# Shorter assignment rounds, whole-pass rejection and evenly spaced gathers in a fused transform and mixture-of-experts kernel

## Chip, cores, metric

One core of a Trainium2 chip. The metric is the device time of one execution in microseconds (us). A time is a median over runs; "span" is the length of one profiled execution, about 1.9 us under its time. Engines carry the profile's names: PE is TensorE, PEld its weight loads, DVE VectorE, ACT ScalarE, POOL GpSimd.

## The reference, cut to what matters

```python
x = real(fft2(x))                       # (8, 2496, 256) -> 19968 tokens of 256
logits = x @ w_gate                     # 8 experts
cap = N // E                            # 2496 tokens per expert
for idx in argsort(-logits.flatten()):  # best score first
    tok, e = idx // E, idx % E
    if assigned[tok] < 0 and counts[e] < cap:
        assigned[tok] = e; counts[e] += 1
for e in range(E):
    out[assigned == e] = relu(x[assigned == e] @ w1[e]) @ w2[e]
```

The greedy assignment is the awkward part. The kernel replaces the sorted walk by rounds: every token proposes to its best expert that has not rejected it, every expert over its capacity rejects its lowest proposals, and so on until nobody is over.

## The kernel before

Tokens that are certain after a first pass are processed as 40 "early" tiles (five per expert, 384 tokens each). The assignment of the others runs beside these tiles, step by step, mostly on VectorE. When it has settled, the rows of the remaining tokens are known, and 16 "late" tiles follow; their token rows are fetched from HBM by indirect transfers that GpSimd issues. GpSimd also writes all output rows, again by indirect transfers. Of a tile:

```python
def gather(d):                       # a late tile: three indirect transfers
    ...
    for q in range((d["n"] + P - 1) // P):
        nc.gpsimd.indirect_dma_start(out=xg[0:nr, q, :], in_=t_dram,
                                     in_offset=IndirectOffsetOnAxis(ap=d["ids"](q, nr), axis=0))

def up(d, fcs):                      # hps: 128 x 384, two matmuls each, evicted by ACT or DVE (take)
    ...
def down(d, b0, group):              # ops: 8 matmuls, evicted into a ring of output tiles, then put
    ...
    ot = out_tile()                  # ring of 8; of 18 once the assignment has settled
    take(ot[0:nr, :], ops[0:nr, 0:D])
    put = nc.gpsimd.indirect_dma_start(out=out, out_offset=..., in_=ot[0:nr, :])
```

What drives the assignment is a generator. It yields the VectorE time that a step costs, or SYNC, and `pace` takes a few steps after each third of a tile. A SYNC (a "break") ends this step, so that the PE work of a third of a tile lies between a VectorE result and the matmul that reads it. When the generator ends at tile j, `settled(j)` notes that tile, and `feed` starts the gathers at the next one:

```python
def pace(j):
    credit[0] = min(credit[0] + 1.9, CREDIT)
    while credit[0] > 0.0 and not placed:
        c = next(todo, "end")
        if c == "end":
            settled(j)                        # placed = [j]; wider ring; deeper PSUM buffers
            return
        if c is SYNC:
            return
        credit[0] -= c
        ...
def feed(j):
    ...
    while m < len(late) and placed and j >= min(max(placed[0] + 1 + (3 * m) // 2, 0 if m < 8 else 32), 38 + m):
        gather(late[m])
        ...
```

In the profile's lines hps and ops are the two matmul groups of a tile, sps those that sort tokens into tiles, inv_ps the inverse permutation that finds the late rows, trun, s_part and lists_x the assignment's thresholds, search and lists, xg, xl and xs the fetched rows, tp their transposes; zball holds output tiles and weights; dd and wa hold output tiles once the assignment has settled.

A round is `choose` (reject and pick the best expert), `lowest` (the eight lowest proposals per partition and expert), `search` (a search for the threshold by comparing 1,024 elements per turn) and `settle`.

## Time and profile before

| | before |
|---|---|
| time, median of the first 3 runs | 548.45 us (547.43 to 548.97) |
| span of the profile that the prediction reads | 591.5 us |
| span of a second profile of the same kernel, taken later | 546.0 us |
| PE, DVE, ACT, POOL busy in the second | 467.9, 386.9, 345.6, 312.1 us |

The two profiles differ by 45 us. The first comes from an execution of 593.3 us, far slower than the timed ones, and the prediction, which had only that one, says so. The second profile (run b_again below) is of the timed kind; all comparisons with the changed kernel use it. Here are the span, GpSimd's slices (40 of 13.7 us, busy tenths) and the last line of its chain of work that ended last:

```profile
span 546.0 us, 11322 instructions
...
PE   0576759797799999999899959999999999999970
...
POOL 7888814443131754544344423467777777777775
...
DMA out_dram<-zball,rows_l 0%; POOL out_dram L1256 0%; POOLq L1347 0%
```

Three things are to be seen. PE is at 9 nearly throughout from the twelfth slice on, and idle in the last one. POOL stands at 7 from slice 28 to slice 39, never higher or lower. And the chain ends on a put of POOL (out_dram), not on PE, though it is cut off there. A constant 7 fits a queue that is always busy but has a fixed pause between its instructions (0.97 of every 1.28 us, as the timeline shows). The timeline of the same kernel (start, duration, engine, line, operation, in brackets the idle time before and what ended it) shows the first gather, the last PE work and the last puts:

```profile
358.83 1.01 POOL L1205 DMA_INDIRECT xg<-t_dram,ids_l  x1 [0.30 <-issue]
...
524.67 3.66 PE L1252 MATMUL ops<-w2t,hb 128*128 128x256 bf16 x32
...
528.37 0.38 ACT L990 ACTIVATE zball<-ops 96x256 f32<-96x256 f32 x1 [1.36 <-PE ops L1252]
...
539.40 0.97 POOL L1256 DMA_INDIRECT out_dram<-zball,rows_l  x1 [0.30 <-DMA out_dram<-zball,rows_l]
540.68 0.93 POOL L1256 DMA_INDIRECT out_dram<-zball,rows_l  x1 [0.30 <-DMA out_dram<-zball,rows_l]
```

PE has finished at 528.33, the last eviction (ACT, 528.37) at 528.75, and the put of that tile starts at 540.68, 11.9 us later. Each transfer takes POOL 0.97 us and a pause of 0.30. This is the backlog that the argument turns on.

### The profile page before, as it was taken

The page shows a single profiled execution, that of the slowest core. Times are in us where ns is not written, and L with a number is a line of the kernel's source. Part 1 is how long each engine was busy: PE and PEld are TensorE (multiplying, and loading weights), DVE is VectorE, ACT ScalarE, POOL GpSimd, SP SyncE. Part 2 cuts the span into 40 slices and gives each one's busy share as a digit, 9 for nine tenths or more (in the row PEclk, how much of TensorE's full clock was granted, in tenths as well). Part 3 has the DMA queues.
Part 4 walks back from the last instruction along what each step waited for, and adds up shares of the span by engine and source line. Part 5 has one row for each costly group of instructions (what it writes and reads, how often), then busy time and mean ns, then how long its engine had stood idle before and what let it go on. Part 6 is the DMA issues. An engine that isn't in the chain of part 4 may idle for free. (4 is left out here: it accounts for less than half of the span.)

```text
span 591.5 us, 11322 instructions
## 1 busy us (share of the span) xinstructions
PE 482.5 (82%) x4014; PEld 358.1 (61%) x4023; DVE 383.4 (65%) x1063; ACT 341.7 (58%) x786; POOL 310.8 (53%) x362
## 2 busy tenths in 40 slices
PE   0567778887899999998998798887787679687993
PEld 0444447775686667766765676655565457465772
DVE  7799864978889889798888762543332324343551
ACT  7789861454688778786777476443432334343551
POOL 7878540622226545343444245665666575656553
PEclk9998779999999999999999799999998989989997
DMA  8999835387698962222222223212222221112111
GB/s 270 314 282 305 252 62 83 109 292 207 203 280 162 240 148 90 91 94 89 89 90 95 69 89 98 71 54 76 66 65 70 67 75 55 61 53 66 65 55 48
DMA packets 35169, 74.63 MB, mean 126 GB/s; under 512 B 6115, under 2 KB 14349, under 8 KB 35104
## 3 DMA queue, kind: packets, MB, share of 16 engines
q0 software_dynamic: 23296, 42.10, 27.4%
q1 hardware_dynamic: 11808, 31.73, 15.9%
q8 instruction: 33, 0.54, 0.4%
q14 instruction: 32, 0.26, 0.1%
HBM read 51.26 MB, written 32.24 MB: 141 GB/s over the span
## 5 line engine op out<-in xcount | busy, mean ns | idle before, releaser
L990 ACT ACTIVATE hb<-hps 128x384 bf16<-128x384 f32 (+1 forms) x331 | 145.8, 492 | 77.1 <-PE hps L1229 61.0
L1252 PE MATMUL ops<-w2t,hb 128*128 128x256 bf16 (+1 forms) x1344 | 178.1, 277 | 0.1
L1252 PEld LDWEIGHTS <-hb 128*128 128x128 bf16 (+1 forms) x1344 | 134.3, 100 | 35.2 <-issue 1.9
L1256 POOL DMA_INDIRECT out_dram<-zball,rid x94 | 96.2, 1024 | 109.6 <-ACT zball L990 96.2
L1229 PE MATMUL hps<-xs,zball 128*128 128x384 bf16 x640 | 131.5, 330 | 19.3 <-issue 10.5
L1229 PEld LDWEIGHTS <-zball 128*128 128x128 bf16 x896 | 86.6, 99 | 87.0 <-issue 48.2
L994 DVE TENSOR_SCALAR hb<-hps 128x384 bf16<-128x384 f32 (+1 forms) x117 | 62.4, 546 | 69.4 <-PE hps L1229 45.2
L1229 PE MATMUL hps<-xt,zball 128*128 128x384 bf16 (+1 forms) x256 | 51.4, 329 | 16.8 <-issue 10.9
L990 ACT ACTIVATE zball<-ops 128x256 f32<-128x256 f32 x96 | 36.9, 385 | 46.8 <-PE ops L1252 26.0
L129 POOL DMA_INDIRECT xb<-in_x_dram,mir_i x40 | 53.0, 1326 | 14.0 <-issue 10.8
L285 PE MATMUL tp<-identf,xa 128*128 128x128 f32 x160 | 28.6, 345 | 21.2 <-issue 11.6
L990 ACT ACTIVATE xs<-sps 128x384 bf16<-128x384 f32 x73 | 32.4, 493 | 20.0 <-PE sps L1093 11.5
L285 PEld LDWEIGHTS tp<-identf,xa 128*128 128x128 f32 x160 | 24.2, 180 | 28.8 <-issue 13.9
L1093 PE MATMUL sps<-pt,xl 128*128 128x192 bf16 x320 | 34.4, 248 | 2.8 <-DVE pt L1071 1.8
L1021 POOL COPY stage<-stage 128x258 bf16<-128x258 bf16 x40 | 17.7, 446 | 35.8 <-DVE stage L1016 32.6
L1071 DVE TENSOR_SCALAR pt<-rampw,spot 128x193 bf16<-128x193 bf16 x160 | 32.2, 293 | 1.0 <-PE sps L1093 0.7
L1093 PEld LDWEIGHTS <-xl 128*128 128x128 bf16 x320 | 27.5, 99 | 8.1 <-issue 6.0
L1256 POOL DMA_INDIRECT out_dram<-zball,rows_l x23 | 22.3, 971 | 17.0 <-DVE zball L996 9.9
L996 DVE COPY zball<-ops 128x256 f32<-128x256 f32 (+1 forms) x21 | 8.9, 423 | 30.0 <-PE ops L1252 9.6
L1205 POOL DMA_INDIRECT xg<-t_dram,ids_l x24 | 23.1, 964 | 7.9 <-issue 7.9
L1019 ACT ACTIVATE stage<-stage 128x254 bf16<-128x254 bf16 x40 | 15.7, 414 | 15.8 <-DVE stage L1016 13.9
L287 ACT COPY zt<-tp 128x1024 f32<-128x1024 f32 (+1 forms) x24 | 20.2, 868 | 6.1 <-PE tp L285 6.1
(357 smaller groups left out, 783.5 us busy)
## 6 DMA issues: line engine op xcount, KB each, us to landing
t_dram<-stage SPq DMA_DIRECT2D x20, 512.0 KB
xl<-t_dram SPq DMA_DIRECT2D x20, 512.0 KB
xa<-in_x_dram SPq DMA_DIRECT2D x8, 1024.0 KB
w1raw<-in_moe_w_dram POOLq DMA_DIRECT2D x8, 512.0 KB
w2t<-in_moe_w_dram POOLq DMA_DIRECT2D x8, 512.0 KB
xa<-in_x_dram SPq DMA_DIRECT2D x8, 224.0 KB
out_dram<-zball,rid POOLq DMA_INDIRECT x94
xb<-in_x_dram,mir_i POOLq DMA_INDIRECT x40
```

What stands on the lines that cost most here:

```text
L129: nc.gpsimd.indirect_dma_start(out=bv[0:n, i, :], out_offset=None, in_=x_pairs, in_offset=bass.IndirectOffsetOnAxis(ap=mir_i[0:n, b * NK + ...
L285: nc.tensor.transpose(tp[:, blk, u, :], pv[:, 4 * c + u, blk * P:(blk + 1) * P], identf)
L287: nc.scalar.copy(zt[:, :, 0:nn, :], tp[:, :, 0:nn, :])
L990: nc.scalar.activation(dst, src, ACT.Relu if relu else ACT.Copy)
L994: nc.vector.tensor_scalar(dst, in0=src, scalar1=0.0, scalar2=None, op0=AL.max)
L1021: nc.gpsimd.tensor_copy(st[:, :, 1 + q, 0:P + 1], st[:, :, 3 * q, 0:P + 1])
L1071: nc.vector.tensor_scalar(marks[n][:, f, 0:EW + 1], in0=rampw[:, 0:EW + 1], scalar1=spot[:, c:c + 1], scalar2=None, op0=AL.is_equal)
L1093: nc.tensor.matmul(sps[:, j2 * EW:(j2 + 1) * EW], lhsT=xl[:, 2 * g + cc, j2 * P:(j2 + 1) * P], rhs=pt[:, 2 * g + cc, 0:EW], start=(cc == 0 ...
L1205: nc.gpsimd.indirect_dma_start(out=xg[0:nr, q, :], out_offset=None, in_=t_dram, in_offset=bass.IndirectOffsetOnAxis(ap=d["ids"](q, nr), ax ...
L1229: nc.tensor.matmul(hps[:, 0:n], lhsT=w1t[d["e"]][:, j2, fc * P:(fc + 1) * P], rhs=d["x"](j2), start=(j2 == 0), stop=(j2 == 1))
L1252: nc.tensor.matmul(ops[0:nr, 0:D], lhsT=d["hid"][:, fc, b0:b0 + nr], rhs=w2t[d["e"]][:, fc, :], start=(fc == 0), stop=(fc == F // P - 1))
L1256: put = nc.gpsimd.indirect_dma_start(out=out, out_offset=bass.IndirectOffsetOnAxis(ap=d["rows"](b0 // P)[0:nr], axis=0), in_=ot[0:nr, :], ...
```

## The change

Its intent is a shorter assignment beside the tiles:

- Rejection and choice are two whole passes over 8 x 160 elements instead of eight steps of 160 each. The choices are marked in bf16 and counted by ten PE matmuls rather than by VectorE's accumulator.
- From the second round on, lists of four per partition instead of eight, and two search turns instead of three; the first round loses its third search turn.
- 56 leftover tokens per partition instead of 64; the inverse permutation is computed in a layout with an inner run of eight, and gets one more break before its first matmul.
- Gathers are spread evenly from the settled tile to tile 52, in place of two in every three tiles.

```diff
 def choose(first):
-    for e in range(E):
-        nc.vector.tensor_scalar(wa[:, e, :], in0=lg[:, e, :], scalar1=tsel[:, e:e + 1], scalar2=0.0,
-                                op0=AL.add, op1=AL.min)
-        ...
-    nc.vector.scalar_tensor_tensor(wa, in0=wa, scalar=K_PEN, in1=lg, op0=AL.mult, op1=AL.add)
+    nc.vector.tensor_tensor(off, lg, tsel[:, :, None].to_broadcast([P, E, GC]), op=AL.is_lt)
+    nc.vector.scalar_tensor_tensor(wa, in0=off, scalar=-K_PEN, in1=lg, op0=AL.mult, op1=AL.add)
     ...
-    for e in range(E):
-        nc.vector.scalar_tensor_tensor(dd[:, e, :], in0=src[:, e, :], scalar=0.0, in1=mx, op0=AL.add,
-                                       op1=AL.is_lt, accum_out=cnt[:, e:e + 1])
-        ...
+    nc.vector.tensor_tensor(off, src, mx[:, None, :].to_broadcast([P, E, GC]), op=AL.is_lt)

 def count():
-    nc.tensor.matmul(cps[:, 0:1], lhsT=cnt_x, rhs=onesf, start=True, stop=True)
+    for c in range(0, GC, NG):
+        nc.tensor.matmul(cps[:, 0:P], lhsT=onesb, rhs=off[:, :, c:c + NG], start=(c == 0), stop=(c + NG == GC))

 def settle_rest():
-    yield from finish_round()            # search(1), then settle()
+    yield from settle()
     for _ in range(NROUND - 1):
-        yield from round_steps()         # lists of eight, search(3)
+        yield from round_steps(4, 2)

 # the inverse permutation
     yield SYNC
+    if c0 == 0:
+        yield SYNC
 # the eight keys of a step
-    yield 0.6
+    yield 0.75

 def feed(j):
-    ... placed[0] + 1 + (3 * m) // 2 ...
+    ... placed[0] + 1 + m * (51 - placed[0]) // 15 ...
```

(Cut: the penalty constant, raised from 1e16 to 1e20, other raised yields, the narrower lists in `lowest`, the inner-eight layout of the inverse, and the renaming of `dd` to `off`, a bf16 view of the same buffer, which the profile goes on calling dd.)

More of the change, by code (lines that the diff above doesn't have):

```diff
@@ L34 @@
 MAGIC = 12582912.0
-K_PEN = 1.0e16
+K_PEN = 1.0e20
 K_LOW = 1.0e30
@@ L53 @@
 CB = 20
-KC = 64
+KC = 56
 OT = 8
@@ L519 @@
     dd = asg.tile([P, E, GC], FT, name="dd")
+    off = dd.rearrange("p e c -> p (e c)").bitcast(BF)[:, 0:E * GC].rearrange("p (e c) -> p e c", c=GC)
     ohb = asg.tile([P, E, GC], BF, name="ohb")
@@ L522 @@
     tree = asg.tile([P, 4, GC], FT, name="tree")
-    cnt = asg.tile([P, E], FT, name="cnt")
     lists = asg.tile([P, E, 8], FT, name="lists")
     lists_x = asg.tile([P, 8, P], FT, name="lists_x")
-    cnt_x = asg.tile([P, P], FT, name="cnt_x")
+    cjunk = asg.tile([P, P], BF, name="cjunk")
     tsel = asg.tile([P, E], FT, name="tsel")
@@ L582, in choose @@
         else:
-            for e in range(E):
-                nc.vector.tensor_scalar(wa[:, e, :], in0=lg[:, e, :], scalar1=tsel[:, e:e + 1], scalar2=0.0,
-                                        op0=AL.add, op1=AL.min)
-                if e % 2 == 1:
-                    yield 0.5
-            nc.vector.scalar_tensor_tensor(wa, in0=wa, scalar=K_PEN, in1=lg, op0=AL.mult, op1=AL.add)
-            yield 1.4
+            nc.vector.tensor_tensor(off, lg, tsel[:, :, None].to_broadcast([P, E, GC]), op=AL.is_lt)
+            yield 1.5
+            nc.vector.scalar_tensor_tensor(wa, in0=off, scalar=-K_PEN, in1=lg, op0=AL.mult, op1=AL.add)
+            yield 1.5
             src = wa
@@ L595, in choose @@
         nc.vector.tensor_tensor(mx, mx, mv, op=AL.max)
-        yield 1.0
-        for e in range(E):
-            nc.vector.scalar_tensor_tensor(dd[:, e, :], in0=src[:, e, :], scalar=0.0, in1=mx, op0=AL.add,
-                                           op1=AL.is_lt, accum_out=cnt[:, e:e + 1])
-            if e % 3 == 2:
-                yield 1.05
-        nc.vector.tensor_copy(cnt_x.rearrange("p (e g) -> p e g", g=NG), cnt[:, :, None].to_broadcast([P, E, NG]))
-        yield 0.9
+        yield 1.2
+        nc.vector.tensor_tensor(off, src, mx[:, None, :].to_broadcast([P, E, GC]), op=AL.is_lt)
+        yield 1.5
         chosen["src"] = src
@@ L607, in count, with lowest @@
         cps = misc()
-        nc.tensor.matmul(cps[:, 0:1], lhsT=cnt_x, rhs=onesf, start=True, stop=True)
-        nc.vector.tensor_scalar(exc, in0=cps[:, 0:1], scalar1=-1.0, scalar2=float(P * GC - CAP), op0=AL.mult, op1=AL.add)
+        for c in range(0, GC, NG):
+            nc.tensor.matmul(cps[:, 0:P], lhsT=onesb, rhs=off[:, :, c:c + NG], start=(c == 0), stop=(c + NG == GC))
+        less = small("less")
+        nc.vector.scalar_tensor_tensor(cjunk, in0=cps[:, 0:P], scalar=-1.0, in1=bdiag, op0=AL.mult, op1=AL.mult,
+                                       accum_out=less)
+        nc.vector.tensor_scalar(exc, in0=less, scalar1=float(P * GC - CAP), scalar2=None, op0=AL.add)
     chosen, found = {}, {}
-    def lowest():
-        nc.vector.scalar_tensor_tensor(wa, in0=dd, scalar=-K_LOW, in1=chosen["src"], op0=AL.mult, op1=AL.subtract)
-        yield 1.4
+    def lowest(deep_):
+        nc.vector.scalar_tensor_tensor(wa, in0=off, scalar=-K_LOW, in1=chosen["src"], op0=AL.mult, op1=AL.subtract)
+        yield 1.5
+        step = 32 // deep_
         for e in range(E):
@@ L618, in lowest @@
             if e % 4 == 3:
-                es = slice(e - 3, e + 1)
-                nc.vector.tensor_copy(lists_x.rearrange("p j (e g) -> p j e g", g=NG)[:, :, es, :],
-                                      lists[:, es, :].rearrange("p e j -> p j e")[:, :, :, None].to_broadcast(
-                                          [P, 8, 4, NG]))
-                yield 1.8
+                yield 1.3
+            if (e + 1) % step == 0:
+                es = slice(e + 1 - step, e + 1)
+                nc.vector.tensor_copy(lists_x.rearrange("p j (e g) -> p j e g", g=NG)[:, 0:deep_, es, :],
+                                      lists[:, es, 0:deep_].rearrange("p e j -> p j e")[:, :, :, None].to_broadcast(
+                                          [P, deep_, step, NG]))
+                yield 0.5
         yield SYNC
         count()
-        lt = psr[0].tile([P, 8, P], FT, tag="lt", bufs=1, name="lt")
-        for j in range(8):
+        lt = psr[0].tile([P, deep_, P], FT, tag="lt", bufs=1, name="lt")
+        for j in range(deep_):
             nc.tensor.transpose(lt[:, j, :], lists_x[:, j, :], identf)
@@ L633, in lowest @@
         nc.vector.tensor_reduce(hi0, lt[:, 0, :], axis=AXX, op=AL.max)
-        nc.vector.tensor_reduce(lo0, lt[:, 7, :], axis=AXX, op=AL.max)
+        nc.vector.tensor_reduce(lo0, lt[:, deep_ - 1, :], axis=AXX, op=AL.max)
         wid = small("wid")
         nc.vector.tensor_tensor(wid, hi0, lo0, op=AL.subtract)
-        yield 0.7
-        found["low"], found["wid"], found["lo0"] = lo0, wid, lo0
+        yield 1.2
+        found["low"], found["wid"], found["lo0"], found["n"] = lo0, wid, lo0, deep_ * P
     def search(turns):
-        junk = wa.rearrange("p e c -> p (e c)")[:, 0:8 * P]
+        junk = wa.rearrange("p e c -> p (e c)")[:, 0:found["n"]]
         for _ in range(turns):
@@ L654, in search @@
             nc.vector.tensor_scalar(wid2, in0=part, scalar1=1.001, scalar2=None, op0=AL.mult)
-            yield 2.0
+            yield 0.9 + found["n"] / 850.0
             yield SYNC
@@ L665, in settle @@
         low, wid, lo0, ltf = found["low"], found["wid"], found["lo0"], found["ltf"]
-        junk = wa.rearrange("p e c -> p (e c)")[:, 0:8 * P]
+        junk = wa.rearrange("p e c -> p (e c)")[:, 0:found["n"]]
         top = small("top")
@@ L670, in settle @@
         nc.vector.tensor_scalar(junk, in0=ltf, scalar1=top, scalar2=0.0, op0=AL.is_gt, op1=AL.add, accum_out=n_top)
-        yield 1.5
+        yield 0.4 + found["n"] / 850.0
         nc.vector.scalar_tensor_tensor(junk, in0=junk, scalar=-1.0e34, in1=ltf, op0=AL.mult, op1=AL.add)
-        yield 1.2
+        yield 0.1 + found["n"] / 900.0
         best = small("best", 8)
         nc.vector.max(best, junk)
-        yield 1.1
+        yield 0.1 + found["n"] / 900.0
         left_ = small("left")
@@ L687, in settle @@
         nc.vector.tensor_tensor(trun, trun, tnew, op=AL.min)
-        yield 1.0
+        yield 1.6
         yield SYNC
@@ L691, in settle, with round_steps @@
         nc.tensor.transpose(bps[:, 0:P], trun.to_broadcast([P, P]), identf)
-        nc.vector.tensor_copy(tsel, bps[:, 0:P:NG])
+        nc.vector.tensor_scalar(tsel, in0=bps[:, 0:P:NG], scalar1=-1.0, scalar2=None, op0=AL.mult)
         yield 0.2
-    def finish_round():
-        yield from search(1)
-        yield from settle()
-    def round_steps():
+    def round_steps(deep_, turns):
         yield from choose(False)
-        yield from lowest()
-        yield from search(3)
+        yield from lowest(deep_)
+        yield from search(turns)
         yield from settle()
@@ L753, in inverse @@
             yield 0.65
-            o_hi = moe.tile([P, 8, EW + 2], BF, tag="pt", bufs=2, name="o_eq")[:, :, 0:w]
-            nc.vector.tensor_tensor(o_hi, rampw[:, None, 0:w].to_broadcast([P, 8, w]),
-                                    hi1[:, cs, None].to_broadcast([P, 8, w]), op=AL.is_equal)
-            nc.vector.tensor_tensor(o_hi, o_hi, pay[:, cs, None].to_broadcast([P, 8, w]), op=AL.mult)
-            yield 0.9
+            o_eq = moe.tile([P, 8, EW + 2], BF, tag="pt", bufs=2, name="o_eq")
+            if w <= P:
+                o_hi = o_eq.rearrange("p a b -> p (a b)")[:, 0:8 * w].rearrange("p (h c) -> p h c", c=8)
+                nc.vector.tensor_tensor(o_hi, ramp8[:, 0:w, :], hi1[:, None, cs].to_broadcast([P, w, 8]),
+                                        op=AL.is_equal)
+                nc.vector.tensor_tensor(o_hi, o_hi, pay[:, None, cs].to_broadcast([P, w, 8]), op=AL.mult)
+                o_hi = o_hi.rearrange("p h c -> p c h")
+            else:
+                o_hi = o_eq[:, :, 0:w]
+                nc.vector.tensor_tensor(o_hi, rampw[:, None, 0:w].to_broadcast([P, 8, w]),
+                                        hi1[:, cs, None].to_broadcast([P, 8, w]), op=AL.is_equal)
+                nc.vector.tensor_tensor(o_hi, o_hi, pay[:, cs, None].to_broadcast([P, 8, w]), op=AL.mult)
+            yield 0.8
             yield SYNC
+            if c0 == 0:
+                yield SYNC
             for c in range(8):
@@ L838, in first_strips @@
         nc.vector.scalar_tensor_tensor(sure, in0=mv, scalar=0.0, in1=sure, op0=AL.is_le, op1=AL.mult)
-        nc.vector.scalar_tensor_tensor(ohb, in0=dd, scalar=0.0, in1=sure[:, None, :].to_broadcast([P, E, GC]),
+        nc.vector.scalar_tensor_tensor(ohb, in0=off, scalar=0.0, in1=sure[:, None, :].to_broadcast([P, E, GC]),
                                        op0=AL.is_le, op1=AL.mult)
@@ L887, in first_chain @@
         yield from choose(True)
-        yield from lowest()
+        yield from lowest(8)
         yield from search(2)
@@ L898, in choose_rest @@
         count()
-        nc.vector.scalar_tensor_tensor(ohb, in0=dd, scalar=0.0, in1=rest[:, None, :].to_broadcast([P, E, GC]),
+        nc.vector.scalar_tensor_tensor(ohb, in0=off, scalar=0.0, in1=rest[:, None, :].to_broadcast([P, E, GC]),
                                        op0=AL.is_le, op1=AL.mult)
@@ L1318, in feed @@
             settled(j)
-        while m < len(late) and placed and j >= min(max(placed[0] + 1 + (3 * m) // 2, 0 if m < 8 else 32), 38 + m):
+        while m < len(late) and placed and j >= min(max(placed[0] + 1 + m * (51 - placed[0]) // 15, 0 if m < 8 else 32), 38 + m):
             gather(late[m])
@@ L1348 @@
         for _ in range(FALLBACK_ROUNDS):
-            run(round_steps())
+            run(round_steps(8, 3))
         run(choose(False))
@@ L1356 @@
             with tc.For_i(0, FALLBACK_LOOP):
-                run(round_steps())
+                run(round_steps(8, 3))
         run(choose_rest())
```

## The prediction

> **What bounds the kernel now.** I read the page first (busy shares and the forty slices), then the chain of work that ended last, then TensorE's waits by stretch, then the timeline of the one stretch where TensorE is weak, and last the groups of instructions of VectorE by shape.
>
> ```profile
> PE 482.5 (82%) x4014; PEld 358.1 (61%) x4023; DVE 383.4 (65%) x1063; ACT 341.7 (58%) x786; POOL 310.8 (53%) x362
> ...
> PE   0567778887899999998998798887787679687993
> ...
> DVE  7799864978889889798888762543332324343551
> ...
> PE 29%; issue 6%; POOL 2%; another core or an unknown queue 1%; ACT 1%; DVE 1%; POOLq 0%
> ```
>
> TensorE is the busiest engine and the chain that ended last runs along it: of what that chain names, 29% is TensorE and 1% VectorE. The row of slices (14.8 us each) has TensorE mostly at 9 from about 160 to 310 us, while VectorE, which works off the token assignment beside the experts, stays at 6 to 9 until about 355 us and then falls to 2 to 5. So the assignment, which is what this change rewrites, lies beside TensorE's matmuls. It costs time only where TensorE stands still for it.
>
> ```profile
> PE misc L658 <- DVE s_part L652: 2.1, 3, 1.1
> PE sps L1093 <- DVE pt L1071: 1.3, 2, 0.7
> PE lt L628 <- DVE lists_x L620: 0.8, 1, 0.8
> PE misc L691 <- DVE trun L687: 0.8, 1, 0.8
> ...
> PE inv_ps L761 <- DVE o_eq L757: 5.4, 1, 5.4
> ```
>
> These are TensorE's waits from 240 to 320 us (the first four; with two of 0.5 and 0.4 us for the slot scan they come to 5.9 us) and from 320 to 358 us (the last). They are all waits for VectorE's assignment. The largest single one is the first matmul of the inverse permutation. Its surroundings in the timeline:
>
> ```profile
> 322.03 1.04 PE L1252 MATMUL ops<-w2t,hb 128*128 128x256 bf16 x8
> ...
> 328.46 0.64 PE L761 MATMUL inv_ps<-o_eq,oh 128*128 128x48 bf16 x8 [5.40 <-DVE o_eq L757]
> ...
> 328.93 1.45 PE L1093 MATMUL sps<-pt,xl 128*128 128x192 bf16 x8
> ...
> 330.18 2.08 PE L1229 MATMUL hps<-xs,zball 128*128 128x384 bf16 x6
> ...
> 337.72 1.14 PE L1229 MATMUL hps<-xs,zball 128*128 128x384 bf16 x6
> ```
>
> After the 5.40 us hole, six hps matmuls take 2.08 us where six of them later take 1.14. The profile's loss in this place is therefore the hole plus about 1.6 us (0.94 there, and 0.6 in the sps group before it, which takes 0.82 us elsewhere).
>
> One warning on this profile: it spans 591.5 us, the timed runs take 548.45. The tiles between about 360 and 545 us are uneven in it (some start 5.3 us after the one before, some 10 us), the last five come every 5.3 to 5.5 us. If I add up 56 tiles at 5.45 us (305), 16 sorting calls of two groups at 0.82 us (26), four weight transposes of 3.4 (14), four row sums at 0.7 (3) and some 23 us of the assignment's own matmuls, and put them after the 173.8 us at which the first tile starts, I get 545. The timed run is close to that without any of those uneven gaps. So I take them for something that the profiled execution has and the timed one mostly lacks, and expect nothing from them.
>
> [...]in the table by stretches (each engine's busy time and count, then clock, DMA share and GB/s) the hole's stretch has a granted clock of 0.83 and its neighbours 1.00, and the matmuls above take almost twice as long.
>
> ```profile
> 300.00:320.00 20.00, 18.41 (x141) 13.34 (x142) 16.69 (x60) 14.70 (x37) 9.63 (x10) 1.00 0.26 85
> 320.00:340.00 20.00, 14.60 (x126) 11.32 (x125) 16.64 (x51) 10.21 (x25) 5.49 (x5) 0.83 0.18 61
> 340.00:360.00 20.00, 19.50 (x200) 15.38 (x200) 11.35 (x43) 14.78 (x38) 8.50 (x9) 1.00 0.25 83
> ```
>
> [...]
> [...]1,280 fp32 elements take 1,511 ns (the L588 group), while bf16 1,024 elements whose broadcasts keep an inner run of 8 take 685 ns (L751). But 384 bf16 elements with the broadcast on the inner dimension take 555 ns (L755)[...].
> [...]Here 160 elements take 302 to 320 ns, and an eighth of the 1,511 ns would be 189. That is the argument for whole passes.
> [...]
>
> **The change part by part.**
> VectorE. (1) Rejection and choice, five times over (the first without rejection): eight steps of 302 ns, eight counting steps of about 0.26 us start to start and a 0.27 us spread go; two passes of 1,280 elements at about 1.45 us (an estimate from the 1,511 and 1,483 ns rows) come. About 4.2 us become 2.9 in four of them, 2.4 become 1.45 in the first: 6 us saved. (2) The count now reads 128 columns from PSUM and reduces them: about 0.35 us more, five times, 1.7 lost. (3) Search: a turn takes 2.26 us in the timeline, of which 1,284 ns is the comparison of 1,024 elements; at 512 that is about 750 ns[...], so 1.73 a turn. Ten turns after the first strips become six: 22.6 less 10.4, 12 saved. (4) Settling on 512 elements in three rounds: three passes less 0.53 us each, 4.8 saved. (5) One spread copy of 434 ns less in three rounds: 1.3. (6) 56 keys for 64: one max and replace (0.7) and one chunk of eight of the inverse (1.8) less. (7) The inverse's two 384-element steps go to the inner-8 layout: 555 to about 357 ns, twice in seven chunks, 2.8 saved. Together 28 us of VectorE's 383. All of it lies beside TensorE.
> TensorE. Each count becomes ten matmuls of 128 columns[...] in place of one fp32 one (about 0.14)[...]. Twelve fp32 transposes less (eight take 1.07 us): 1.5 saved. Four search matmuls and eight inverse ones less: 0.9. Net 1 us more, on the path.
> Waits. The inverse gets one more break before its first matmul. A break lasts one third of a tile, 1.85 us between ops groups, and the yields before it are raised to what VectorE really needs (0.75 for 0.6 at each key step, 1.6 for 1.0 at the end of settling), so that VectorE is less behind when TensorE gets there. I expect 1 to 2 us to be left of 5.4, so 4 saved, and the 1.6 of slow clock with it. Of the other 5.9 us of waits in 240 to 320 us, the searching and settling ones should about halve, as there are 27 breaks for 31 and each has less VectorE work before it: 3 saved.
> Order. Stepping through the builder, the assignment ends at tile 20 and not at 24 (74 paced steps become some 60), so the deeper PSUM buffers and the wider ring of output tiles come four tiles sooner. TensorE idles little in those tiles, so half a microsecond. The gathers start at tile 21 and come every second tile to 52, instead of two in three from 25 to 47: GpSimd issues 4.5 instead of 5 indirect transfers a tile. At the 1.28 us spacing of such issues in the trace that is 5.8 us against 6.4, for a tile of 5.45; the ring of 18 output tiles takes up a lag of this kind. I put 1 us on it.
> First stage (100 to 175 us): about 0.6 us less VectorE work net, and TensorE's waits for it are short: 0.3.
> Sum: 4 + 1.6 + 3 + 0.5 + 1 + 0.3 less 1 is 9.4 us. [...]I take four fifths, 7.5: 548.45 becomes 541.
>
> Is the shortened assignment still complete? If it were not, the kernel would run its fallback[...]. I replayed both versions' rounds on the reference's scores: with four per partition, the second round rejects 112 of expert 7's surplus of 116, the third makes good, and after four rounds both versions end with no surplus. The fullest partition has 52 tokens left over, under 56. So no fallback.
>
> **The rivals.** (a) Nothing happens: VectorE was beside the path, and TensorE's added counts eat the small waits. For it speaks the chain (VectorE 1%); against it the 5.4 us hole, which is on TensorE in the middle of its busy stretch. It would give 545 to 549. (b) GpSimd is the true limit after tile 25: its indirect transfers stand back to back at 1.28 us while gathers run, and spreading them lifts a limit that the timed run has too. For it speak the uneven tiles of the profile; against it that adding up the work already gives the timed length. It would give 528 to 537. (c) The hole moves: with the assignment ending four tiles sooner, the same wait comes under a heavier load of sorting, or the ten count matmuls, which now wait on a whole pass, become a new hole of 1 to 2 us each. It would give 545 to 552; the raised yields speak against it.
>
> **Range and chances.** My middle is 541. (a) and half of (c) lie within 2%; 537.5 is the border to faster, and only (b), or all waits going at full value, gets there. I take 534 to 547.5 as the range for 8 in 10, faster by over 2% at 0.2, within 2% at 0.77, slower at 0.03.
>
> **What would show it.** Right: TensorE's wait at the inverse's first matmul under 2 us and the clock in that stretch at 1.00; the assignment's last VectorE step some 25 us sooner than 354.6; VectorE about 28 us less busy in all[...]. Wrong: a tail of tiles evenly faster after 360 us would mean rival (b); new waits of TensorE on the lines of the count would mean (c); a gain far over 9 us means that I undersized what the waits cost in the timed run; none at all means that the hole was made by the profile.

## The result, and the profile after

| | before | after |
|---|---|---|
| time, median | 548.55 us (547.43 to 548.97, 4 runs) | 535.99 us (535.51 to 536.25, 4 runs) |
| ratio of fast runs, 95% interval | | 0.9773 (0.9756 to 0.979) |
| span of the profile | 546.0 us (second profile) | 534.3 us |
| granted PE clock | 0.962 | 0.969 |
| DVE busy | 386.9 us | 372.7 us |

A ratio is the mean time of one kernel's fast runs over that of the other's fast runs of the same rounds, so it is not quite the ratio of the medians. The changed kernel is 2.3% faster: in the predicted range (534 to 547.5), 5 us under its middle, and just over the 2% line to which the prediction had given 0.2.

The same rows of the page, now of the changed kernel, with its chain:

```profile
span 534.3 us, 11232 instructions
...
PE   0567659899789899999899999999999999999983
...
POOL 7888815253122555555524336777677777777774
...
PE 70%; DVE 13%; ACT 9%; issue 4%; DMA 3%; POOL 1%; POOLq 0%; DVEq 0%; ACTq 0%
```

POOL's stretch of sevens begins two slices earlier (26 instead of 28, in slices of 13.4 us instead of 13.7), and the chain that ended last now runs along PE. The timeline answers to the lines shown of before:

```profile
328.16 1.01 POOL L1210 DMA_INDIRECT xg<-t_dram,ids_l  x1 [0.31 <-issue]
...
526.85 0.97 POOL L1261 DMA_INDIRECT out_dram<-zball,rows_l  x1 [0.30 <-issue]
528.13 0.93 POOL L1261 DMA_INDIRECT out_dram<-zball,rows_l  x1 [0.30 <-issue]
```

The first gather goes out at 328.16 instead of 358.83. The last put starts at 528.13, 1.5 us after its eviction instead of 11.9. PE itself ends at 526.19, only 2.1 us before the 528.33 of before, so most of the gain in these two spans cannot be PE's. PE's waits from 180 to 345 us (what waited, on what; total, count, longest, us) are these:

```profile
PE misc L601 <- DVE dd L594: 2.7, 1, 2.7
PE misc L690 <- DVE trun L686: 2.1, 1, 2.1
PE sps L1098 <- DVE pt L1076: 0.7, 2, 0.5
```

The 5.4 us wait before the inverse is gone. Two waits have taken its place in part: the ten count matmuls of the choice for the leftover tokens (the "second pass" of the expectations) wait 2.7 us for a whole VectorE pass, and the first settling waits 2.1 us. After the first the clock is lower, too: 0.91 from 260 to 280 us, with 1.00 in the 20 us before and after:

```profile
262.87 1.14 PE L1234 MATMUL hps<-xs,zball 128*128 128x384 bf16 x6
...
267.62 0.72 PE L601 MATMUL misc<-dd,onesb 128*128 128x128 bf16 x10 [2.74 <-DVE dd L594]
...
269.04 2.13 PE L1234 MATMUL hps<-xs,zball 128*128 128x384 bf16 x6
```

Six hps matmuls take 1.14 us before this hole and 2.13 us after it. In the second half, where b_again has no PE wait at all, two late gathers now hold PE:

```profile
PE tp L1222 <- DMA xs<-t_dram,ids_l: 2.3, 2, 1.4
```

Where the 11.7 us of the spans come from can be read along POOL's queue, because in the kernel before its transfers stand without a break from the first gather to the last put: 143 of them, (540.68 - 358.83) / 142 = 1.281 us apart.

| step | us |
|---|---|
| first gather, 358.83 to 328.16 | -30.7 |
| 155 transfers from there instead of 143 (12 more puts now fall after the first gather), 12 x 1.281 | +15.4 |
| pauses in the queue: 528.13 - 328.16 = 199.97, full it would be 154 x 1.281 = 197.3 | +2.7 |
| last put to end of span, 5.3 to 6.2 | +0.8 |
| sum | -11.7 |

The first gather is 30.7 us sooner because the assignment ends at tile 20 and not at tile 24 (tile 21 starts 24.3 us before tile 25, at 324.1 and 348.4) and because the tiles themselves come 6.4 us sooner (tile 25 at 348.4 instead of 354.85), as the hole before the inverse (5.4 us) and the slow clock after it (0.83 from 320 to 340 us in b_again, 1.00 here) are gone. This is arithmetic on two traces, and no two traces start alike: the first tile (its first hps matmul) starts at 171.5 us in b_again and at 172.1 here, and in the six kernels that share the same code up to that tile (this one and five below) it starts anywhere from 170.3 to 173.4. Differences of 1 to 3 us between two single traces are therefore read from the first tile, where that matters. Whether POOL's queue sets the end, and what each part of the change is worth, needed experiments.

### The profile page after: what moved, and what is told of

The parts are those of the page before. It is cut to its first block, busy times and chain, and to the rows that moved or that the text cites. A ratio compares the mean times of both kernels' runs of the same rounds, so it can differ in the third digit from the quotient of the medians.

```text
span 534.3 us, 11232 instructions
## 1 busy us (share of the span) xinstructions
PE 471.8 (88%) x4039; PEld 357.7 (67%) x4039; DVE 372.7 (70%) x952; ACT 337.9 (63%) x762; POOL 313.9 (59%) x362
## 4 chain that ended last, share of the span: by engine, by line
PE 70%; DVE 13%; ACT 9%; issue 4%; DMA 3%; POOL 1%; POOLq 0%; DVEq 0%; ACTq 0%
PE hps L1234 24%; PE ops L1257 24%; PE sps L1098 5%; PE fftps L1038 5%; PE wps L1058 2%; PE tp L285 2%; ACT zt L287 2%; DMA xa<-in_x_dram 2%; PE yps L295 1%; ACT tf L254 1%; POOL out_dram L1261 1%; DVE xa L343 1%; PE inv_ps L766 1%; DVE stage L1022 1%; PE tp L1222 1%
## 5 line engine op out<-in xcount | busy, mean ns | idle before, releaser
L1257 PE MATMUL ops<-w2t,hb 128*128 128x256 bf16 (+1 forms) x1344 | 175.3, 274 | 0.0
L1261 POOL DMA_INDIRECT out_dram<-zball,rid x85 | 89.3, 1051 | 82.7 <-ACT zball L995 63.8
L1234 PE MATMUL hps<-xs,zball 128*128 128x384 bf16 x640 | 127.3, 327 | 0.0
L999 DVE TENSOR_SCALAR hb<-hps 128x384 bf16<-128x384 f32 (+1 forms) x122 | 66.3, 549 | 47.2 <-PE hps L1234 39.2
L129 POOL DMA_INDIRECT xb<-in_x_dram,mir_i x40 | 54.3, 1357 | 11.9 <-issue 10.5
L995 ACT ACTIVATE zball<-ops 128x256 f32<-128x256 f32 (+1 forms) x79 | 30.4, 384 | 31.6 <-PE ops L1257 29.0
L1234 PE MATMUL hps<-xt,zball 128*128 128x384 bf16 (+1 forms) x256 | 48.4, 322 | 0.0
L995 ACT ACTIVATE xs<-sps 128x384 bf16<-128x384 f32 x68 | 30.4, 493 | 16.0 <-PE sps L1098 15.7
L1044 ACT COPY ev<-fftps 128x512 f32<-128x512 f32 x20 | 11.7, 584 | 22.9 <-PE fftps L1038 15.5
L1001 DVE COPY zball<-ops 128x256 f32<-128x256 f32 (+1 forms) x29 | 12.3, 424 | 19.4 <-PE ops L1257 19.4
```

The costliest lines, as they stand in the source:

```text
L129: nc.gpsimd.indirect_dma_start(out=bv[0:n, i, :], out_offset=None, in_=x_pairs, in_offset=bass.IndirectOffsetOnAxis(ap=mir_i[0:n, b * NK + ...
L995: nc.scalar.activation(dst, src, ACT.Relu if relu else ACT.Copy)
L999: nc.vector.tensor_scalar(dst, in0=src, scalar1=0.0, scalar2=None, op0=AL.max)
L1234: nc.tensor.matmul(hps[:, 0:n], lhsT=w1t[d["e"]][:, j2, fc * P:(fc + 1) * P], rhs=d["x"](j2), start=(j2 == 0), stop=(j2 == 1))
L1257: nc.tensor.matmul(ops[0:nr, 0:D], lhsT=d["hid"][:, fc, b0:b0 + nr], rhs=w2t[d["e"]][:, fc, :], start=(fc == 0), stop=(fc == F // P - 1))
L1261: put = nc.gpsimd.indirect_dma_start(out=out, out_offset=bass.IndirectOffsetOnAxis(ap=d["rows"](b0 // P)[0:nr], axis=0), in_=ot[0:nr, :], ...
```

## The experiments

Theory A: from the first gather on, GpSimd's queue of indirect transfers sets the end. A change in the assignment counts through the moment of the first gather. Theory B: TensorE sets the end, and the change counts by the holes that it takes out of TensorE. All runs gave correct results. In the expectations quoted below, the letters stand for what each text itself says.

**b_again: the kernel before, unchanged.** To see whether the first profile stands for the timed runs.

> The kernel before, unchanged, to have its profile a second time. If the uneven tiles of the first profile belong to how this kernel is profiled, the profile spans about 590 us again; if they were a chance event of one execution, it spans about 547 us and shows the timed run as it is. The timed runs are 548 us either way.

Measured: 548.41 us (18 runs), ratio 0.9997, span 546.0 us. The tiles from 360 us on start 5.2 to 5.9 us apart except for one step of 6.6, where the first profile has steps of 5.2 to 10.5. The uneven tiles do not belong to the timed kernel.

**b_even: the kernel before with the even spacing alone.**

```diff
-    ... placed[0] + 1 + (3 * m) // 2 ...
+    ... placed[0] + 1 + m * (51 - placed[0]) // 15 ...
```

> The kernel before with the evenly spaced gathers alone (tiles 25 to 52 in place of 25 to 47). Theory A, the gain comes from TensorE's waits for the assignment: within 1 us of 548. Theory B, GpSimd's queue of indirect transfers runs late after tile 25 and the gathers' spacing decides how late: 541 to 545 us.

Measured: 551.46 us, ratio 1.0069 (1.0052 to 1.0086), 0.7% slower: clear of the noise, though under the 2% that counts as slower. Neither theory expected it. The puts are prompt at the end (the last one 1.5 us after its eviction), but PE now waits, from 480 us on:

```profile
PE tp L1217 <- DMA xs<-t_dram,ids_l: 7.8, 5, 3.7
```

The last gathers are issued late into a queue that is full all the same, and PE stands for them and ends at 540.3 us instead of 528.3. The queue runs from 360.3 to 542.18 us, 143 transfers at 1.281: full in both orders. Spreading the gathers does not relieve the queue. It only decides whether puts or gathers are late. What makes the time longer is not shown by these traces: of the 2.3 us of span, 1.4 are a later first gather, up to which the two kernels are the same, and 0.8 lie after the last put.

**b_break: the kernel before with the additional break and the key share of 0.75.**

```diff
     yield SYNC
+    if c0 == 0:
+        yield SYNC
...
-    yield 0.6
+    yield 0.75
```

> The kernel before with the one more break before the inverse's first matmul and the key steps' yields at 0.75, nothing else. Theory A: the 5.4 us hole shrinks to 1 to 2 us and the clock stays up, 542 to 544 us. Theory B: under 2 us gained, 546.5 to 548.5 us.

Measured: 543.49 us, ratio 0.9921 (0.9904 to 0.9937). The wait falls from 5.4 us to this:

```profile
PE inv_ps L763 <- DVE o_eq L757: 1.9, 1, 1.9
```

The assignment still ends at tile 24, but the first gather goes out at 354.6 instead of 358.8, and with the same 143 transfers the last put starts at 536.21 instead of 540.68. The last put is again 11.8 us behind its eviction. So removing the hole brings 4.9 us in the median and 4.5 in the span, and both theories can claim it: PE ends 4.3 us sooner (524.01), and the queue as much. (The first tile happens to start 1.8 us later here, at 173.3; counted from there, both gain 6 us.)

**a_oldg: the changed kernel with the old gather spacing.** The b_even diff, reversed.

> The changed kernel with the old spacing of the gathers (tiles 21 to 43). Theory A: 535 to 537 us as the changed kernel. Theory B: 539 to 543 us, as GpSimd has 5 transfers a tile and falls behind by a microsecond a tile. A third possibility, that the last gather of the changed kernel is late and the old spacing avoids it: 532 to 534 us.

Measured: 533.59 us (530.79 to 535.42), ratio 0.9723 (0.9681 to 0.9765), in the range of the third possibility. The interval touches that of the changed kernel (0.9756 to 0.979), so the gain of half a per cent is likely but not settled by itself; b_even points the same way. PE has no wait from 480 us on, and the tiles keep their 5.2 to 5.6 us to the end. The queue is full: 155 transfers from 329.53 to 526.53, 1.279 us apart.

**a_rounds8, a_dup, a_nobreak and a_fix fell on another chip (number 5 in the record; the other experiments ran on 15, 8 and 6).** On it the kernel before takes 599.2 us (592.2 to 606.1, 39 runs), and its times spread by over 2%, so times of this group are not compared with the others. Three of the kernels were run again. What these runs do show is told first.

a_rounds8 (the changed kernel, old spacing, old rounds):

```diff
+    yield from search(1)
     yield from settle()
     for _ in range(NROUND - 1):
-        yield from round_steps(4, 2)
+        yield from round_steps(8, 3)
```

> The changed kernel with the old gather spacing, and with the old rounds put back (lists of eight, one search step): everything else of the change stays. The assignment then ends at tile 23 instead of 20 and the gathers start at tile 24 instead of 21. Theory A (GpSimd's backlog sets the end: what the rounds of four bring is an earlier start of the gathers): the last transfers come late again, the stretch from the last tile's start to the end grows from 17.9 us to about 22 or 23, and the time is 538 to 541 us against 533.6 of the same kernel with rounds of four. Theory B (the rounds only lie beside TensorE, their length costs nothing): 532 to 535 us.

a_dup (the changed kernel, old spacing, each late tile's first 128 rows fetched twice):

```diff
 def gather(d):
+    nc.gpsimd.indirect_dma_start(out=xg[0:P, 0, :], in_=t_dram,
+                                 in_offset=IndirectOffsetOnAxis(ap=d["ids"](0, P), axis=0))
     for q in range((d["n"] + P - 1) // P):
```

> The changed kernel with the old gather spacing, in which each of the 16 gathers' first 128 rows are fetched twice into the same place: 16 more indirect transfers on GpSimd's queue, the result unchanged. Theory A (GpSimd's queue of indirect transfers is full from tile 21 to the end): each adds its 1.285 us to the end, 16 x 1.285 = 20.6 us, so 551 to 555 us, with the last put far behind its eviction. Theory B (TensorE alone sets the end and the puts only trail by their latency): less than 3 us more, below 537 us.

a_nobreak (the changed kernel, even spacing, without the break):

```diff
     yield SYNC
-    if c0 == 0:
-        yield SYNC
...
-    yield 0.75
+    yield 0.6
```

> The changed kernel without the additional break ahead of the inverse's first matmul and with the old key share of 0.6; the rounds of four, the whole passes and the even spacing stay. Theory A (the break took away the hole, which also lowered the granted clock): a wait of 3 to 6 us before the inverse's matmul is back at about the 14th to 22nd tile, and the time is 538 to 542 us against 536 for the changed kernel. Theory B (the hole vanished because the rounds of four leave VectorE less loaded, the break is not needed): no such wait, 535 to 537 us.

a_fix (the changed kernel, old spacing, one break more):

```diff
 def choose_rest():
     yield from choose(False)
     yield SYNC
+    yield SYNC
     count()
```

> The changed kernel with the old gather spacing and with one more break: choose_rest's count matmuls are issued one tile later than the whole pass on VectorE that they read. Theory A (the 2.7 us hole at the second pass is on the path, as TensorE is full before it): the wait for dd is gone or below 0.5 us, and the time falls from 533.6 to 529 to 532 us. Theory B (GpSimd's queue is the true limit of the end, tiles before it have slack): the wait is gone, but the gathers start no earlier, and the time stays at 532.5 to 535 us.

Measured: a_rounds8 595.9 us (ratio 0.9987, 0.9955 to 1.002), a_dup 621.6 (one run), a_nobreak 602.35 (1.0043, 1.0011 to 1.0075), a_fix 591.92 (0.9868, 0.9819 to 0.9917). None of the times expected for the faster chip could be met here. The traces of this group have the look of the first profile, whose execution of 593.3 us lies in this chip's range, with tiles 5 to 13 us apart once the gathers run. In that first profile one such place reads:

```profile
446.09 0.55 DVE L994 TENSOR_SCALAR hb<-hps 128x384 bf16<-128x384 f32 x1
...
447.19 0.49 ACT L990 ACTIVATE hb<-hps 128x384 bf16<-128x384 f32 x1 [3.70 <-PE hps L1229]
447.54 0.98 POOL L1256 DMA_INDIRECT out_dram<-dd,rid  x1 [0.30 <-issue]
447.89 0.49 PE L1229 MATMUL hps<-xs,zball 128*128 128x384 bf16 x2
450.08 0.38 ACT L990 ACTIVATE zball<-ops 128x256 f32<-128x256 f32 x1 [2.40 <-remote]
```

From 447.7 to 450.1 VectorE and ScalarE stand still together (VectorE from 446.6), though the matmuls whose results they then evict had ended by 448.4; PE waits in turn. There are at least seventeen such common stops of 1.2 to 2.6 us in the first profile between 400 and 590 us, and in b_again none before PE's end. It is not that transfers are slower: in both traces the last DMA packet of an indirect transfer ends a median 1.1 to 1.2 us after POOL is done with it. The trace of the slow kind does hold only half as many records of landed transfers (244 on one queue's semaphore, against 528 in b_again). No run here shows why the engines stop, and the cause stays open. It is not needed for the change: the timed comparison was made where before takes 548 us.

The waits before 320 us, ahead of the gathers, can still be read. In a_nobreak:

```profile
PE misc L601 <- DVE dd L594: 2.7, 1, 2.7
...
PE inv_ps L764 <- DVE o_eq L754: 1.9, 1, 1.9
```

Without the break the wait before the inverse is 1.9 us, where 3 to 6 were expected: most of the old 5.4 us went with the rest of the change (lighter rounds, whole passes, the inner-eight layout; which of them is not separated), and the break takes the remaining 1.9. In a_fix the dd wait is gone. In a_rounds8 it is 1.2 us, but the search waits are back with 3.1 us in five.

**a_dup_again.** The decisive run for theory A, now where before takes 548.84 us.

> The kernel of the run a_dup once more, as that run fell on a chip on which the kernel before takes 599 us and not 548. On a chip on which before takes about 548: theory A (GpSimd's queue of indirect transfers is full from tile 21 to the end, so each of the 16 added ones moves the end by its 1.285 us): 551 to 556 us, no hps wait longer than before up to the gathers, and a put lag that grows to the end. Theory B (TensorE alone sets the end): below 537 us. If it falls on a slow chip again: 618 to 625 us.

Measured: 554.16 us (553.13 to 556.36), ratio 1.011, against 533.59 for the same kernel without the 16 transfers. That is 20.6 us, and 16 x 1.285 is 20.6. The agreement to a tenth is luck, as the runs of the two kernels spread by 3.2 and 4.6 us. The traces say it more closely: from the first gather to the last put it is 218.0 us here and 197.0 in a_oldg, 21.0 us for 16 more transfers. Each added transfer moved the end by its full place in the queue. Theory B's "below 537" is out. 171 transfers stand 1.282 us apart from 326.27 to 544.25. The backlog of puts grows until, at 460 us, all 18 output tiles of the ring wait for their put, 33 us behind. An ops tile can then not be evicted, and PE stops:

```profile
PE ops L1260 <- ACT wa L995: 4.6, 2, 3.3
PE ops L1260 <- ACT zball L995: 3.4, 1, 3.4
```

**a_rounds8_again.** What the rounds of four bring, everything else of the change being present.

> The kernel of the run a_rounds8 once more, as that one fell on a chip on which before takes 599 us. Compared with the 533.6 us of the same kernel with rounds of four (ratio to before 0.972). Theory A (GpSimd's queue of indirect transfers is full from the first gather to the end, as the 16 added transfers moved the end by 20.6 us; what the rounds of four bring is that the first gather goes out three tiles earlier): three tiles of 5.9 us later is some 17 us of queue time, of which the slack that the queue had at the end of the kernel with rounds of four is taken first; 538 to 543 us, ratio 0.980 to 0.990, and the stretch from the last tile's start to the end 22 us or more against 17.9. Theory B (the rounds only cost their waits): 532 to 535 us, ratio 0.969 to 0.975, last stretch unchanged.

Measured: 541.68 us (541.42 to 541.97), ratio 0.9875 (0.9853 to 0.9897), 8.1 us over a_oldg and in theory A's range. Its timeline and the last line of its chain:

```profile
348.07 1.01 POOL L1211 DMA_INDIRECT xg<-t_dram,ids_l  x1 [0.31 <-issue]
...
534.20 0.93 POOL L1262 DMA_INDIRECT out_dram<-zball,rows_l  x1 [0.30 <-DMA out_dram<-zball,rows_l]
```

```profile
DMA out_dram<-zball,rows_l 0%; POOL out_dram L1262 0%; POOLq L1353 0%
```

The last tile starts at 515.6 us, in a_oldg at 515.5, and PE ends at 523.38 against 523.27. That looks as if the rounds of four saved TensorE nothing, but the first tile starts at 170.6 us here and at 173.4 in a_oldg, with the same code up to it. Counted from the first tile, they save TensorE 2.9 us and bring the first gather forward by 21.4. As the two traces stand, the first gather comes 18.5 us sooner (348.07 to 329.53), at the price of nine more transfers behind it (11.5 us), and the last put moves by 7.7 us. The last put is 10.4 us behind its eviction here, 2.8 in a_oldg. Theory B could claim the 2.9 us; the times differ by 8.1.

**a_nobreak_again.**

> The kernel of the run a_nobreak once more, on a chip as the changed kernel had it, if one comes. On the slow chip its wait ahead of the inverse was 1.9 us and not the 5.4 of before, so the expectation of the first time, 538 to 542 us, is too high in its own terms. Theory A (the break brings only what that wait is, as most of the old hole went with the lighter rounds): 536 to 538 us against the 536.0 of the changed kernel, with a wait of about 1.9 us at the inverse. Theory B (GpSimd's queue sets the end, and without the break the assignment ends one tile sooner, so the gathers start sooner): 533 to 536 us in spite of the wait.

Measured: 539.63 us (539.17 to 539.79), ratio 0.9837 (0.9815 to 0.9859): 3.6 us over the changed kernel, above both theories' ranges. PE's waits from 180 to 345 us:

```profile
PE misc L601 <- DVE dd L594: 2.7, 1, 2.7
PE misc L690 <- DVE trun L686: 2.1, 1, 2.1
PE inv_ps L764 <- DVE o_eq L754: 1.9, 1, 1.9
PE sps L1096 <- DVE pt L1074: 1.4, 1, 1.4
```

The break, with the raised yields that go with it, is worth more than the wait it takes away. The wait is 1.9 us, but VectorE is late for the sorting matmuls too (1.4 instead of 0.7), and the clock between 300 and 320 us is 0.92 instead of 1.00, so that tile 22 starts 4.2 us later than in the changed kernel (334.2 and 330.0; 0.4 of it from the first tile on). The first gather goes out one tile earlier in the program and only 1.5 us earlier in time, with three more transfers behind it. By the queue that is 3 x 1.28 - 1.5 = 2.3 us later, and the last put is indeed 2.1 us later (530.25 and 528.13).

**a_fix2: the changed kernel, old spacing, one more break ahead of each of the two new waits.** a_fix's break, and:

```diff
 # settle, before its transpose
     yield SYNC
+    if found["n"] > 4 * P:
+        yield SYNC
```

> The changed kernel with the old gather spacing and two more breaks, one ahead of the choice's count matmuls in the second pass and one ahead of the first settling's counts, so that both waits that the change had opened (2.7 and 2.1 us) lie over a tile's matmuls. Both waits should be gone or below 0.5 us. On a chip on which before takes about 548 the changed kernel with the old spacing took 533.6: theory A (these waits are on the path) 528 to 531 us, a ratio to before of 0.963 to 0.968; theory B (they are made up at the end, where GpSimd's queue is the limit) 532 to 535 us. On a slow chip the waits can still be read, the time not.

Measured: 532.05 us (530.61 to 533.28), ratio 0.9692 (0.966 to 0.9723). PE's waits in the same stretch:

```profile
PE misc L692 <- DVE trun L686: 1.1, 1, 1.1
PE lt L627 <- DVE lists_x L619: 1.0, 2, 0.6
```

The 2.7 us wait is gone, the 2.1 us one is halved only, and 1.0 us has opened at the lists. The first gather comes at 325.9, 3.6 us before a_oldg's (1.2 of it because the first tile starts sooner), the queue stays full (155 transfers, 1.280 us apart) and the last put comes 3.5 us sooner; the span is 2.7 us shorter. The median, 1.5 us under a_oldg's, falls in theory B's range, but the two intervals overlap, and a_oldg's four runs split into pairs near 531 and 535. So what these waits are worth is not settled. Against the changed kernel the intervals are apart: this is the fastest version found, 3.1% under the kernel before by its ratio, and some 0.7% under the changed one by the medians, 532.05 and 535.99.

The runs of the faster kind together; "computed" is the first gather plus (transfers - 1) x 1.281 us:

| kernel | time, us | first tile | first gather | transfers | last put computed | last put | PE ends |
| --- | --- | --- | --- | --- | --- | --- | --- |
| b_again | 548.41 | 171.5 | 358.8 | 143 | 540.7 | 540.7 | 528.3 |
| b_even | 551.46 | 172.2 | 360.3 | 143 | 542.2 | 542.2 | 540.3 |
| b_break | 543.49 | 173.3 | 354.6 | 143 | 536.5 | 536.2 | 524.0 |
| a_rounds8_again | 541.68 | 170.6 | 348.1 | 146 | 533.8 | 534.2 | 523.4 |
| a_oldg | 533.59 | 173.4 | 329.5 | 155 | 526.8 | 526.5 | 523.3 |
| a_fix2 | 532.05 | 172.2 | 325.9 | 155 | 523.2 | 523.0 | 519.7 |
| a_dup_again | 554.16 | 170.3 | 326.3 | 171 | 544.0 | 544.3 | 533.3 |
| changed kernel | 535.99 | 172.1 | 328.2 | 155 | 525.4 | 528.1 | 526.2 |
| a_nobreak_again | 539.63 | 172.5 | 326.6 | 158 | 527.8 | 530.3 | 526.8 |

In seven of nine the queue is full from first to last and computed and measured agree within 0.4 us. The two others are the ones with the changed kernel's even spacing: their queue has pauses of 2.5 to 2.7 us in all, as the gathers come too sparsely at first, and the last ones hold PE. Between the last put and the end lie 5.3 to 7.7 us, different from kernel to kernel, in which the profile counts no instruction. The DMA record has the last output data there, done 1.7 to 3.4 us after the last put's start, and otherwise only transfers of instructions: one in the three kernels with 5.3 us, two to six in the others. The two go together; that the one causes the other was not tested.

The table also gives the parts of the change, as steps between medians: the break takes the kernel before to 543.49 us (b_break); the whole passes, the 56 leftovers, the inner-eight layout and the other yields, which have no run of their own, to 541.68 (a_rounds8_again, 1.8 us by difference, the intervals of the two ratios just apart); the rounds of four to 533.59 (a_oldg); and the even spacing back to 535.99.

## Why the prediction was right, and by which steps it was not

The total, 541 for a measured 536, was right within its range, and the hole at the inverse was a true part of it. But several terms of its sum were not right, and the largest effect had one of the smallest terms. That the sum of 9.4 us, cut to 7.5 by the author's estimate, came as near as it did to 12.5 is in part luck.

- **The check that dismissed rival (b).** The prediction added up tiles, sorting and assignment to 545 us and took the closeness to 548 as evidence against GpSimd as the limit. In the profile of the timed kind PE ends at 528.3 us; the last put at 540.7 and 5.3 us more make up the span. The sum came out at the right number with work that TensorE did not have: it has 371 us after the first tile's start, where PE of b_again needs 356.8 (171.5 to 528.3). The four weight transposes take 1.9 us each there and not 3.4, and the recorded matmuls of the assignment add up to 14 us and not 23. The result, 536.0, lies in the range that the prediction gave to rival (b), 528 to 537. That rival was right about the limit and wrong that spreading the gathers lifts it.
- **Order and spacing, 0.5 + 1 us.** These were the mis-sized terms. That the assignment ends at tile 20 was seen correctly, and so were the 1.28 us of an issue. But the value was looked for in deeper buffers and in a thinner stream of gathers. It lay in the earlier first gather: with the rounds of four alone, 8.1 us (a_rounds8_again against a_oldg). The even spacing, to which the 1 us was given, costs: 0.7% in b_even, and about half a per cent in the changed kernel by a_oldg, less surely.
- **The inverse's hole, 4 + 1.6 us.** Right in mechanism and nearly in size. The wait went from 5.4 to nothing, better than the 1 to 2 us expected, and the granted clock is 1.00 in every stretch of 20 us from 280 to 360, where b_again has 0.83 from 320 to 340. The change without the break leaves 1.9 us of it, the break alone leaves 1.9 too; the break in the kernel before is worth 4.9 us.
- **The other waits, 3 us by halving.** Not so. The kernel before has 6.6 us of them between 180 and 358 us (sps, the search, trun, the lists, the slot scan); the changed one has 5.5 between 180 and 345 us, almost all in two places, the 2.7 and the 2.1 us. That is the half of rival (c) about the count matmuls, with 2.7 us in one of five and not 1 to 2 in each.
- **The clock after a short hole.** The prediction counts a slow clock for the 5.4 us hole alone; that shorter ones would cost none was the author's assumption. The 2.1 us hole of the first settling in the changed kernel left the clock at 1.00 (170 to 190 us). But after the 2.74 us hole the hps group took 2.13 us for 1.14, and the granted clock from 260 to 280 us is 0.91; two waits of 1.4 and 1.9 us in a_nobreak_again were followed by a clock of 0.66 from 299 to 304 us (0.92 from 300 to 320); and the two waits for late gathers in the changed kernel, 0.8 and 1.5 us, by 0.79 from 512 to 520 us.
- **TensorE's count matmuls, part of the net 1 us.** Their time in that sum was the author's estimate and came from no trace. Measured 0.72 us for ten in each of the five, the starts 56 ns apart. The first profile shows that spacing too: its transposes at L1217, bf16 matmuls of 128 columns, take 0.50 us for six, of 219 ns each.
- **VectorE, 28 us less.** Its busy time fell by 14.2 us (386.9 to 372.7). Summing its instructions' durations by line, those of the assignment fell by 34.9 us (168.1 to 133.2, overlaps counted twice), but the balance between the evicting engines then gave it 24 more evictions (174 to 198). The author's estimates of single instructions were right: 750 ns for a comparison of 512 elements and 751 measured, 357 for each of an inverse step's two and 357 and 355 measured, 1.45 us for a whole pass and 1.49 measured (the row of 1,511 ns read for it is a scalar_tensor_tensor, the new passes are tensor_tensor). The assignment lay beside TensorE, as predicted, but not beside the path: it decides when the queue starts.
- **The assignment's last step, 25 us sooner.** Measured 30.7 (352.38 to 321.67).
- **What was to show rival (b).** The prediction looked for evenly faster tiles after 360 us. There are none: b_again and the changed kernel both have steps of 5.2 to 5.9 us there, but for one of 6.6 and, in the changed kernel, one of 9.8 us at the late gathers. The sign was the distance between an eviction and its put at the very end, 11.9 us before and 1.5 after.
- **The warning about the profile.** Right that its uneven tiles do not belong to the timed runs, and expecting nothing from them was right. But that profile also hid the full queue: with PE stopping for other reasons, POOL kept up and its chain named it with 2%.

## What to carry to other kernels

If a queue with a fixed place per transfer (here 1.28 us) is full from some moment to the end, the end is that moment plus the number of transfers times the place; work beside the path then counts by when it lets the queue start, not by what the busiest engine waits for it. Look for it as a flat busy share below 100% with equal pauses (here 7 tenths and 0.30 us), and measure how far the last stores lag behind their producers, before adding up the busiest engine's work. And check that the profile that you read is of the same speed as the timed runs, and that two traces start alike before you compare moments in them: here the first tile moved by up to 3.1 us between runs with the same code before it.
